# Weight pieces fetched by fewer DMAs, and half of w1 and w2 converted a step earlier, in an mLSTM cell with a multiplicative FFN

## The chip, the cores and the metric

The kernel runs on one core of a Trainium2 chip, as one program. The metric is the device time of one execution in microseconds; the median of several runs is given, and a profile of one execution goes with it. Times in the text without a unit of their own are microseconds (us) from the start of the profiled span.

## What is computed

An mLSTM cell over 4 batches, 8 heads, 768 time steps and a head size of 40, followed by a feed-forward block without a nonlinearity of its own, on the 3072 tokens:

```python
# mLSTM, per batch and head, t = 0 .. 767
m_new  = np.maximum(f_gate[t] + m, i_gate[t])
f_stab = np.exp(f_gate[t] + m - m_new);  i_stab = np.exp(i_gate[t] - m_new)
C = f_stab * C + i_stab * outer(v[t], k[t])        # 40 x 40
n = f_stab * n + i_stab * k[t]
y[t] = sigmoid(o_gate[t]) * (C @ q[t]) / max(abs(n @ q[t]), 1)

# FFN on x = y, 3072 tokens x 320
a = x @ w1;  b = x @ w2          # 320 x 1024 each
out = (a * b @ w3) @ w_out       # 1024 x 1024, 1024 x 320
```

The attention inputs are float32. The four weights arrive as float64: each value is two 32-bit words in memory, and the kernel makes float32 of them on the chip. So w3 is 8 MB to be read, w_out, w1 and w2 2.6 MB each.

## The kernel before

**Units and steps.** The sequence is cut into 24 units (6 pieces of 128 time steps x 4 batches). A loop over `s`, from 0 to 31, is written out in full (lines 737 to 831). In step `s` the kernel does the cell's matmuls of unit `s`, the outputs of unit `s-1`, brings the result of unit `s-2` into the layout of the FFN (xT), and adds FFN work as lists say: `n_up[s]` blocks of x @ w1 and x @ w2 (`up`, `up_rest`), `n_down[s]` output blocks (`ffn_out`), and from step 19 on a form of the up-projections with seven products in place of eight. The chunkwise cell needs k, q, v and the output gate of a unit; they are called for two steps ahead (`load`, `load_o`). From unit 10 on k and q are fetched by small DMAs in a form that VectorE turns (`load_turned`, 16 DMAs a unit), before that TensorE turns them.

**Weights.** A weight goes through four stations.

1. `fetch` (line 203) calls for a piece of raw 64-bit words by DMAs on SyncE's queue. The pieces stand in one list, `todo` (line 730): ten pieces of w1 and w2 (two halves of columns; in each half w1, w1, w2, w2 and the piece `wr` that holds the last 64 rows of both), eight pieces of w_out ("wo"), and sixteen parts of w3 (8 blocks of 128 rows, each in two parts of 64). `n_fetch[s]` says how many pieces shall have been called for by the end of step `s`; after step 7 it is four more than have been converted. The words go into a tile `raw` of 128 partitions, of which there are four; two pieces use the still unused memory of w3o instead (`idle`).
2. `scale` (line 179): ScalarE scales the high words (line 183) and the low words (line 187).
3. `convert` with `to_f32` (lines 230 and 189): VectorE puts the two together to a float32 (lines 191 and 192). For w3 it also turns 32 x 32 squares (line 241). `n_cvt[s]` says how many pieces are converted in step `s`. From step 9 on (`ahead`) two pieces are scaled a step before they are converted.
4. `fold` and `w3_mm`: TensorE multiplies the block of w3 by w_out into wp (16 matmuls per two parts), and ScalarE stores it as w3o. Since the FFN has no nonlinearity after a * b, w3 @ w_out is made once and used for all tokens.

**How pieces lie.** A piece of w_out is 128 rows that lie in four places of w_out, 32 rows each at distance 256 (`CQ`), one for each square of 32 partitions. A part of w3 is 64 rows; the columns are cut into four quarters, and quarter `j` goes to partitions 32j to 32j+31, with the two groups of 32 rows side by side in a partition. Before, each square of 32 partitions was fetched by its own DMA: 32 rows x 640 words for w_out, 32 rows x 2 groups x 512 words for w3.

**Order.** The instructions of each engine stand in the order in which the code makes them for the whole stretch up to step 32 (`keep_order`, `pinned`); TensorE has its order written out too (`in_order`). So an instruction that waits holds up all that stands behind it on its engine. SyncE issues all loads in one queue; in a step its order is: row of weights U of unit s+3 (`load_u`), k, q, v and gate of unit s+2, the turned loads of unit s+2, then the weight pieces. On ScalarE, the scaling of a step's weights stands at the end of the step, ahead of the copy of xT (line 468), of the evacuations `a_sb` (line 612) and of w3o (line 257) of the next.

Of the kernel before, what the change touches and what calls it, by code (L numbers as in the profile page):

```python
# [16 lines left out]
def kernel(  # L17
# [37 lines left out]
    DM = H * D  # L55
# [104 lines left out]
    wo = const.tile([128, FO, DM], FP, name="wo")  # L160
# [5 lines left out]
    w1_d, w2_d, w3_d, wo_d = (x.bitcast(U32) for x in (moe_w1, moe_w2, moe_w3, moe_w_out))  # L166
# [3 lines left out]
    def raw_tile(n, pieces):  # L170
        raw = idle.pop(0) if idle else wst.tile([128, n, 2], U32, name="raw", tag="raw", bufs=4)
        for r, src in pieces:
            dst = raw[r].rearrange("p n two -> p (n two)")
            if len(src.shape) == 3:
                dst = dst.rearrange("p (m n) -> p m n", m=2)
            nc.sync.dma_start(out=dst, in_=src)
        return raw

# [15 lines left out]
    def cols(c0, n):  # L194
        return slice(2 * c0, 2 * (c0 + n))
# [1 line left out]
    every = slice(0, 128)  # L197

    CQ = DFF // 4
    squares = [slice(32 * j, 32 * (j + 1)) for j in range(4)]  # L200
    pend, scaled = [], []

    def fetch(kind, i, part):

        if kind == "w12":
            c0 = part * CW
            if i < 2 * KF:
                wt, src = ((w1, w1_d), (w2, w2_d))[i // KF]
                ko = i % KF
                dst, pieces = wt[:, ko, c0:c0 + CW], [(every, src[ko * 128:(ko + 1) * 128, cols(c0, CW)])]  # L210
            else:
                dst, pieces = wr[:, c0:c0 + CW], [(slice(j * REM, (j + 1) * REM), src[KF * P:DM, cols(c0, CW)])
                                                  for j, src in enumerate((w1_d, w2_d))]
        elif kind == "wo":
            dst, pieces = wo[:, i, :], [(square, wo_d[j * CQ + i * 32:j * CQ + (i + 1) * 32, :])
                                        for j, square in enumerate(squares)]
        else:
            dst, pieces = None, [(square, w3_d[i * 128 + part * 64:i * 128 + (part + 1) * 64, cols(j * CQ, CQ)]
                                  .rearrange("(m r) n -> r m n", m=2)) for j, square in enumerate(squares)]
        pend.append((dst, raw_tile(dst.shape[-1] if dst is not None else CW, pieces), i, part))  # L220


# [269 lines left out]
    w3o_words = w3o.rearrange("p f d -> p (f d)").bitcast(U32).rearrange("p (n two) -> p n two", two=2)  # L492
    load(0, slice(0, 2))
    fetch("w12", 0, 0)
    load(0, slice(2, 3))
    fetch("w12", 1, 0)
    load(1, slice(0, 2))
    load_o(0)
    load(1, slice(2, 3))
    load_o(1)  # L500
    fetch("w12", 2, 0)
    idle += [w3o_words[:, i * CW:(i + 1) * CW] for i in range(2)]

# [224 lines left out]
    n_down = [0] * 17 + [2] * 6 + [1] * 7 + [0, 5]  # L728
    w12 = [("w12", i, part) for part in range(2) for i in range(2 * KF + 1)]
    todo = w12[3:] + [("wo", i, 0) for i in range(FO)] + [("w3", ko, part) for ko in range(FO) for part in range(2)]  # L730
    n_cvt = [0, 1, 1, 1, 1, 2, 4, 4, 4] + [2] * 7
    n_fetch = [4, 5, 6, 8, 10, 12, 16, 20]
    pinned, ahead = 32, 9
    behind = ExitStack()
    turned, converted, fetched = 0, 2, 3
# [126 lines left out]
```

## Time and profile before

| | |
|---|---|
| time, median of 3 runs | 451.98 us (450.0 to 457.32) |
| span of the profiled execution | 449.5 us |
| 16 DMA engines, share by queue | 50.5% for SyncE's loads (queue 1: 46.29 MB) |
| w3 parts: DMAs, size, issue to landing | 64, 128 KB, 3.3 us (median) |
| w_out pieces: DMAs, size, issue to landing | 32, 80 KB, 2.0 us (median) |
| k, v and gate: DMAs, size, issue to landing | 24 each, 160 KB, 4.5 to 4.8 us (median) |
| fetch of step 5, w_out | 64.26 us, 8 DMAs, 3.89 us of SyncE's time |
| fetch of step 6, w_out | 77.37 us, 16 DMAs, 8.57 us |
| fetch of step 7, w_out and w3 | 93.81 us, 16 DMAs, 3.58 + 4.20 us |
| fetch of step 8, w3 | 110.25 us, 16 DMAs, 8.24 us |
| fetch of step 9, w3 | 128.45 us, 8 DMAs, 3.69 us |
| fetch of step 13, w3, the last | 187.50 us, 8 DMAs, 3.60 us |

The fetches are read from the timeline of SyncE's queue: the first number is when SyncE begins to issue, the last how long it takes over the issues. A DMA's "issue to landing" runs from its own issue to the last of its completion signals. The busy share of the DMA engines is a mean over all 16; the profile doesn't list them one by one.

### The profile page before, as it was taken

The page shows a single profiled execution, that of the slowest core. Times are in us where ns is not written, and L with a number is a line of the kernel's source. Part 1 is how long each engine was busy: PE and PEld are TensorE (multiplying, and loading weights), DVE is VectorE, ACT ScalarE, POOL GpSimd, SP SyncE. Part 2 cuts the span into 40 slices and gives each one's busy share as a digit, 9 for nine tenths or more (in the row PEclk, how much of TensorE's full clock was granted, in tenths as well). Part 3 has the DMA queues.
Part 4 walks back from the last instruction along what each step waited for, and adds up shares of the span by engine and source line. Part 5 has one row for each costly group of instructions (what it writes and reads, how often), then busy time and mean ns, then how long its engine had stood idle before and what let it go on. Part 6 is the DMA issues. An engine that isn't in the chain of part 4 may idle for free.

```text
span 449.5 us, 12899 instructions
## 1 busy us (share of the span) xinstructions
PE 426.9 (95%) x5303; PEld 339.3 (75%) x5303; DVE 299.7 (67%) x629; ACT 150.9 (34%) x410; POOL 81.4 (18%) x155
## 2 busy tenths in 40 slices
PE   4988996999699999999999999999999999999997
PEld 3877875888577878878877878778778777777774
DVE  6375668478827866876685859678698776445800
ACT  4566557268442552353132312203111111001110
POOL 3434433033202211220222203202020000000000
PEclk9987999899989999999999999999999999999999
DMA  8999674569988695788444585563211120000001
GB/s 185 177 174 209 122 142 90 154 148 197 214 188 184 150 191 157 146 169 167 89 95 125 115 162 118 111 131 90 58 36 36 34 50 16 15 16 15 2 30 44
DMA packets 135595, 51.15 MB, mean 114 GB/s; under 512 B 109744, under 2 KB 127344, under 8 KB 135536
## 3 DMA queue, kind: packets, MB, share of 16 engines
q1 hardware_dynamic: 131936, 46.29, 50.5%
q10 hardware_dynamic: 3600, 4.03, 2.5%
q8 instruction: 41, 0.67, 0.6%
q14 instruction: 18, 0.15, 0.1%
HBM read 44.50 MB, written 5.80 MB: 112 GB/s over the span
## 4 chain that ended last, share of the span: by engine, by line
PE 85%; DVE 3%; issue 3%; ACT 3%; POOL 2%; DMA 2%; SPq 1%; POOLq 0%; DVEq 0%; ACTq 0%
PE cell L92 22%; PE pa L92 21%; PE pb L92 14%; PE po L92 14%; PE wp L92 7%; PE p L92 5%; PE pt L95 1%; DMA raw<-in_moe_w_dram 1%; PE px L95 1%; ACT pw L297 1%; POOL pw L302 1%; DMA q_all<-in_q_dram 1%; DVE pw L381 1%; DVE h L412 1%; POOL vw L324 1%
## 5 line engine op out<-in xcount | busy, mean ns | idle before, releaser
L92 PE MATMUL pa<-xT,w 128*128 128x256 f32 x240 | 61.9, 389 | 5.7 <-ACT xT L468 5.7
L92 PE MATMUL po<-w3o,ab 128*128 128x320 f32 x224 | 61.8, 433 | 0.0
L92 PEld LDWEIGHTS pa<-xT,w 128*128 128x128 f32 x240 | 45.4, 194 | 14.0 <-ACT xT L468 6.6
L92 PEld LDWEIGHTS po<-w3o,ab 128*128 128x128 f32 x224 | 42.4, 190 | 17.3 <-issue 0.4
L329 POOL TENSOR_TENSOR state<-state,decay 128x164 f32<-128x164 f32 x40 | 20.9, 523 | 173.9 <-DVE state L388 134.5
L92 PE MATMUL pb<-xT,w 128*128 128x256 f32 x192 | 47.8, 393 | 3.5 <-DVE w L192 3.5
L302 POOL TENSOR_SCALAR_AFFINE_SELECT pw<-pw 64x512 f32<-64x512 f32 x48 | 33.5, 697 | 64.3 <-ACT pw L297 50.9
L92 PEld LDWEIGHTS pb<-xT,w 128*128 128x128 f32 x192 | 37.9, 198 | 9.4 <-DVE w L192 3.9
L92 PE MATMUL cell<-w3o,ab 128*128 128x320 f32 x160 | 44.0, 432 | 0.0
L613 DVE TENSOR_TENSOR ab<-pb,a_sb 128x512 f32<-128x512 f32 x24 | 16.5, 689 | 39.2 <-ACT a_sb L612 39.2
L297 ACT ACTIVATE pw<-pw,aT 128x64 f32<-128x64 f32 x160 | 40.3, 340 | 2.8 <-ACT o_sb L715 2.8
L92 PEld LDWEIGHTS cell<-w3o,ab 128*128 128x128 f32 x160 | 30.4, 190 | 12.0
L612 ACT ACTIVATE a_sb<-pa 128x512 f32<-128x512 f32 x24 | 14.3, 597 | 70.6 <-PE pb L92 70.6
L92 PE MATMUL pa<-xT,wr 64*64 64x256 f32 x384 | 36.8, 386 | 1.1 <-DVE wr L192 1.1
L92 PE MATMUL pb<-xT,wr 64*64 64x256 f32 x384 | 36.2, 379 | 0.0
L660 DVE SCALAR_TENSOR_TENSOR a_sb<-pa,wo 128x512 f32<-128x512 f32 x12 | 8.3, 692 | 41.7 <-PE pa L92 41.7
L92 PE MATMUL wp<-wo,w3T 128*128 128x320 f32 x128 | 35.8, 432 | 0.0
L92 PEld LDWEIGHTS pa<-xT,wr 64*64 64x64 f32 x384 | 19.0, 132 | 16.0 <-issue 8.6
L92 PEld LDWEIGHTS wp<-wo,w3T 128*128 128x128 f32 x128 | 23.7, 190 | 8.9
L715 ACT COPY o_sb<-po 128x320 f32<-128x320 f32 x14 | 6.0, 426 | 67.4 <-PE po L92 63.5
L412 DVE TENSOR_TENSOR h<-cell,h 64x164 f32<-64x164 f32 x76 | 24.8, 326 | 1.4
L92 PEld LDWEIGHTS pb<-xT,wr 64*64 64x64 f32 x384 | 20.2, 133 | 3.0
(135 smaller groups left out, 732.9 us busy)
## 6 DMA issues: line engine op xcount, KB each, us to landing
raw<-in_moe_w_dram SPq DMA_DIRECT2D x64, 128.0 KB, 3.3
kbuf<-in_k_dram SPq DMA_DIRECT2D x24, 160.0 KB, 4.5
vbuf<-in_v_dram SPq DMA_DIRECT2D x24, 160.0 KB, 4.8
o_in<-in_o_gate_dram SPq DMA_DIRECT2D x24, 160.0 KB, 4.7
out_dram<-o_sb ACTq DMA_DIRECT2D x24, 160.0 KB, 1.8
raw<-in_moe_w_dram SPq DMA_DIRECT2D x7, 512.0 KB, 5.1
pw<-U_d SPq DMA_DIRECT2D x28, 128.0 KB, 3.6
raw<-in_moe_w_out_dram SPq DMA_DIRECT2D x32, 80.0 KB, 2.0
```

Source lines behind the costliest of these rows:

```text
L92: in_order(nc.tensor.matmul(out, lhsT=lhsT, rhs=rhs, start=start, stop=stop))
L95: in_order(nc.tensor.transpose(out, in_, ident[0:n, 0:n]))
L297: nc.scalar.activation(out=pw[:, h, :], in_=src[:, h, :], func=AF.Exp, bias=aT[:, c, b * H + h:b * H + h + 1])
L302: nc.gpsimd.affine_select(out=pw[r], in_=pw[r], compare_op=OP.is_ge, fill=0.0, base=0, pattern=[[0, H], [1, L]], channel_multiplier=-1)
L324: nc.gpsimd.tensor_tensor(out=vw_t[n], in0=vbuf[n % NBV], op=OP.mult, in1=wT[:, c, b * H:(b + 1) * H].unsqueeze(2).to_broadcast([P, H, D1]))
L329: nc.gpsimd.tensor_tensor(out=new, in0=old, op=OP.mult, in1=decay[:, b * NP:(b + 1) * NP, 2 * c + x:2 * c + x + 1] .to_broadcast([P, NP, D1]))
L381: first_read = nc.vector.tensor_tensor(out=pv, in0=ss, in1=pv, op=OP.mult)
L412: nc.vector.tensor_tensor(out=part, in0=ph[x][halves[e]], in1=part, op=OP.add)
L612: nc.scalar.mul(out=a_sb, in_=pa, mul=UP ** -2)
L613: nc.vector.tensor_tensor(out=ab_t[gr][j][:, fs[0]:fs[-1] + 1, t0:t0 + a_sb.shape[-1]], in0=pb, in1=a_sb, op=OP.mult)
L660: nc.vector.scalar_tensor_tensor(out=out, in0=p, scalar=UP ** -2, in1=q, op0=OP.mult, op1=OP.add)
L715: nc.scalar.copy(out=o_sb, in_=po)
```

## The change

A piece of w_out is now called for by one DMA in place of four, a part of w3 by two in place of four. The four squares of partitions are filled by one transfer: its destination is all 128 partitions, and its source is a view with the four places (`j`) as its outermost dimension, then 32 rows, then the words of a row. The two DMAs of a w3 part are its two groups of 32 rows. The bytes and the length of the contiguous rows (2,560 and 2,048 bytes) stay as they were. It saves SyncE the issuing of 56 DMAs.

Beside that, `n_cvt` and `n_fetch` are changed so that the second half of w1 and w2 is fetched and converted a step earlier: steps 4 to 6 convert 2, 2 and 3 pieces in place of 1, 2 and 4, and the fetches of steps 2 to 6 each reach one piece further, except that step 6 reaches the same count. From step 7 on both lists are as before.

```diff
     def raw_tile(n, pieces):
         raw = idle.pop(0) if idle else wst.tile([128, n, 2], U32, name="raw", tag="raw", bufs=4)
         for r, src in pieces:
-            dst = raw[r].rearrange("p n two -> p (n two)")
-            if len(src.shape) == 3:
-                dst = dst.rearrange("p (m n) -> p m n", m=2)
+            dst = (raw[:, r] if len(src.shape) == 3 else raw[r]).rearrange("p n two -> p (n two)")
             nc.sync.dma_start(out=dst, in_=src)
         return raw
...
-    squares = [slice(32 * j, 32 * (j + 1)) for j in range(4)]
...
         elif kind == "wo":
-            dst, pieces = wo[:, i, :], [(square, wo_d[j * CQ + i * 32:j * CQ + (i + 1) * 32, :])
-                                        for j, square in enumerate(squares)]
+            dst, pieces = wo[:, i, :], [(slice(0, DM), wo_d.rearrange("(j c) n -> j c n", j=4)[:, i * 32:(i + 1) * 32, :])]
         else:
-            dst, pieces = None, [(square, w3_d[i * 128 + part * 64:i * 128 + (part + 1) * 64, cols(j * CQ, CQ)]
-                                  .rearrange("(m r) n -> r m n", m=2)) for j, square in enumerate(squares)]
+            dst, pieces = None, [(slice(m * CQ, (m + 1) * CQ), w3_d[r0:r0 + 32, :].rearrange("r (j n) -> j r n", j=4))
+                                 for m, r0 in enumerate(range(i * 128 + part * 64, i * 128 + (part + 1) * 64, 32))]
...
-    n_cvt = [0, 1, 1, 1, 1, 2, 4, 4, 4] + [2] * 7
-    n_fetch = [4, 5, 6, 8, 10, 12, 16, 20]
+    n_cvt = [0, 1, 1, 1, 2, 2, 3, 4, 4] + [2] * 7
+    n_fetch = [4, 5, 7, 9, 11, 13, 16, 20]
```

## The prediction

> **What bounds the kernel now.** I read the page from the top (busy time, the 40 slices, the DMA queues), then the chain of waits in order of time, then the waits and the timeline where the chain leaves TensorE, last the windows of the DMA engines.
>
> ```profile
> PE 426.9 (95%) x5303; PEld 339.3 (75%) x5303; DVE 299.7 (67%) x629; ACT 150.9 (34%) x410; POOL 81.4 (18%) x155
> ...
> PE   4988996999699999999999999999999999999997
> ...
> PEclk9987999899989999999999999999999999999999
> DMA  8999674569988695788444585563211120000001
> ```
>
> TensorE is busy for 426.9 of 449.5 us. The dents lie in the first eleven slices (11.2 us each); from about 124 us the digit is 9 up to the tail, so whatever delays TensorE there is added to the time in full, and no change to the loads can gain there. What a faster start can give is bounded by the idle time before 124 us, and two waits in it concern the weights:
>
> ```profile
> PE pb L92 <- DVE w L192: 3.5, 1, 3.5
> ...
> PE pa L92 <- ACT xT L468: 5.7, 3, 4.2
> ...
> ACT raw L183 <- DMA raw<-in_moe_w_dram: 2.8, 3, 1.0
> ```
> ```profile
> 110.25 8.24 SPq L176 DMA_DIRECT2D raw<-in_moe_w_dram  x16
> ...
> 120.51 0.67 ACT L183 ACTIVATE raw<-raw 128x512 f32<-128x512 f32 x1 [0.99 <-DMA raw<-in_moe_w_dram]
> ...
> 123.76 0.46 ACT L468 COPY xT<-px 128x384 f32<-128x384 f32 x1
> ...
> 124.28 2.24 PE L92 MATMUL pa<-xT,w 128*128 128x256 f32 x7 [4.22 <-ACT xT L468]
> ```
>
> The first fence is of the waits (total, times, longest), the second of the timeline (start, us, what). The first wait is at 77.39 us: the second half of w2 isn't converted yet. The second, in step 9, is the interesting one: sixteen DMAs of w3 take SyncE 8.24 us to call for, ScalarE scales each piece when it lands, and behind the last scaling stands the copy of xT for which TensorE waits 4.22 us. The waits of that stage thus end with the landing of w3, and ScalarE is in order, so a later landing moves TensorE one for one.
>
> ```profile
> 113.00:118.00 5.00, 5.00 (x22) 3.79 (x21) 4.43 (x12) 1.25 (x2) 2.64 (x4) 1.00 0.81 221
> 171.00:176.00 5.00, 5.00 (x27) 4.13 (x30) 3.41 (x7) 0.00 (x0) 0.00 (x0) 1.00 0.44 132
> 128.00:143.40 15.40, 15.40 (x210) 12.42 (x209) 11.09 (x23) 6.51 (x17) 3.31 (x6) 0.97 0.84 187
> 143.40:158.80 15.40, 15.40 (x212) 12.48 (x212) 11.36 (x24) 6.50 (x17) 3.32 (x6) 1.00 0.72 172
> 200.00:231.00 31.00, 31.00 (x424) 25.10 (x423) 22.92 (x47) 8.67 (x27) 6.78 (x13) 1.00 0.62 126
> ```
>
> The last two columns are the mean busy share of the 16 DMA engines and GB/s. A step of the steady stage is 15.4 us (the chain of waits has the wp matmuls at 164.74, 180.17 and 195.60 us). The reader is to see that the engines are busy 72 to 84% in a step that fetches two parts of w3 and 62% in steps that fetch none: there is room on sixteen engines, not on a few of them.
>
> **What the Trainium skill says.** (1) "DMA: Bandwidth & Descriptors", section "Why a DMA increments its semaphore by 16 and not by 1": the number of engines k of a DMA is the largest number up to 16 that divides the size of the slowest dimension (other than 1) of both access patterns, and on this path the lowest-numbered k engines are taken. (2) The same page, "Rules for kernel authors": an outermost dimension under 16 confines the whole DMA to that many engines at most. The trace of before agrees as far as it goes:
>
> ```profile
> q1 hardware_dynamic: 131936, 46.29, 50.5%
> q10 hardware_dynamic: 3600, 4.03, 2.5%
> ...
> out_dram<-o_sb ACTq DMA_DIRECT2D x24, 160.0 KB, 1.8
> ...
> gates<-in_i_gate_dram ACTq DMA_DIRECT2D x3, 32.0 KB, 2.0
> ```
>
> Queue 10 carries 24 stores of 128 rows and 3 loads of 32 rows: 24 x (128+16) + 3 x (32+16) = 3600 packets, exactly with 16 completion packets per DMA, so both shapes ran on 16 engines. No DMA of before has an outer size under 32, so no run yet shows k under 16. (3) The page's "Specifications" price one engine at about 27 GiB/s (29 GB/s).
>
> **The change, part by part.**
>
> Fewer DMAs. Before: w_out 8 pieces x 4 and w3 16 parts x 4 = 96 DMAs; after: 8 x 1 and 16 x 2 = 40. SyncE is spared 56 issues of about 0.5 us (8.24 us for 16), some 28 us in all, mostly hidden; in step 9's fetch 4.1 us of issuing goes, which by itself would take away nearly all of the 4.22 us wait.
>
> The shape of those DMAs. Before, both sides of a DMA had 32 outermost. Now the source is 4 x 32 x row (j first) and the destination 128 x row. By (1) and (2) 4 is the largest number dividing 4 and 128, so all of w_out and w3 goes through four engines, which also carry their sixteenth of every other transfer, in the order of one queue. This is the step that decides, so I price it. One part of w3 is 512 KB, 131 KB per engine of the four. At the page's 29 GB/s that is 4.5 us; at what the windows show per busy engine (221/(16 x 0.81) = 17 GB/s, 132/(16 x 0.44) = 18.8) 7.7 to 7.0 us. A third way: two parts raise the engines' busy time per step from 0.62 x 15.4 = 9.5 to (12.9+11.1)/2 = 12.0 us, so 2.5 us for 66 KB, 26 GB/s. I take 25 GB/s, an estimate: 5.2 us a part; a piece of w_out (82 KB per engine) 3.3 us. The other transfers of a step: 9.5 us from the 200 to 231 us window; 7.0 if only its quieter half (215 to 231 us: share 0.44 of 16 us) is taken; I take 9.
>
> So a step with two parts puts 2 x 5.2 + 9 = 19.4 us on the four engines, against 15.4 us of compute: they become the bound. How long: the fetch of step 7 (93.81 us before, about 91 after, the wait of 3.5 us being gone) asks for 2 pieces of w_out and 2 parts of w3, step 8 for 4 parts, steps 9 to 13 for 2 each. To the last landing: 2 x 3.3 + 16 x 5.2 + 6 steps of other loads x 9 = 6.6 + 83.2 + 54 = 143.8 us, so 91 + 143.8 + 2 (landing, as the 2.0 us of w_out on the page) = 236.8 us. In before the last w3 piece is scaled here:
>
> ```profile
> 197.21 0.66 ACT L183 ACTIVATE raw<-raw 128x512 f32<-128x512 f32 x1
> 197.77 0.66 ACT L187 ACTIVATE raw<-raw 128x512 uint32<-128x512 uint32 x1
> 198.34 0.45 ACT L468 COPY xT<-px 128x384 f32<-128x384 f32 x1
> ```
>
> The shift is 236.8 - 197.2 = 39.6 us, gain of the early part included. It builds up so: in step 9 the fourth part lands at 91 + 6.6 + 10.4 + 9 + 20.8 + 2 = 139.8 us where before its scaling began at 122.66, 17 us; then 4 to 5 us in each of five steps (19.4 against 15.4). The ring does not run dry between, since SyncE calls for the next loads right behind each fetch and four raw buffers let two parts stand in the queue while two are converted. Queued behind the waiting scaling on ScalarE are the copy of xT, the evacuations a_sb and the w3o copy; TensorE waits for the first, VectorE (ab) for the second. After step 13 TensorE has no idle time in which to catch up.
>
> The second half of w1 and w2 one step earlier. No instruction more or less, and TensorE's and GpSimd's order is the same; on VectorE one conversion goes from step 6 to step 4. Gain: the 3.5 us wait at 77 us. Cost: one scaling (0.67 + 0.68 us) and conversion (0.85 + 1.0 us) more in step 4, where ScalarE and VectorE have gaps (ScalarE is idle 2.3 us before the kT copy at 58.01), and 512 KB called for one step earlier, at 20 to 40 us, where the DMA engines are full: 512 KB at the 177 GB/s of that stretch is 3 us on loads for k and v. Taken as 0 to 3 us, I take 1, within the rounding of the start at 91.
>
> Sum: 452.0 + 39.6 = 491.6, given as 491.
>
> **The rivals.** (B) Sixteen engines take the new DMAs, if what counts isn't the outermost 4. Then only the gains remain: 3.5 less 1 at 77 us and 4.2 at 124 us: 452.0 - 6.7 = 445.3, faster by 1.5%. For it: that step 9's wait is made of issue time. Against it: the page's rule. (C) Four engines, but hidden: if the rate is 29 GB/s and the other loads cost only 7.0 us, the sum is 2 x 2.8 + 16 x 4.5 + 6 x 7 = 119.6, last landing at 212.6, +15; with another step of slack from the buffers (loads are called for two steps ahead) it ends at 452. Between 450 and 460; against it, the windows' 17 to 19 GB/s. (D) Worse: at 17 GB/s and 9.5 us, 2 x 4.8 + 16 x 7.7 + 57 = 189.8, last landing at 282.8, +85.6: 537; for it, that the windows show this rate under load; against it, that twelve engines fall quiet and contend less.
>
> **How the numbers follow.** Forecast (the four engines bound steps 8 to 13) 0.78; B 0.12; C 0.06; D 0.04. The forecast's own spread follows from the bounds of its two costs, 4.5 to 7.7 us a part and 7.0 to 9.5 us a step, which are unlikely to lie at the same end together: 460 to 530. I give 456 to 532, which holds 0.95 of the forecast and about half of C and D, 0.79 in all, and leaves out B. Slower by over 2% (above 461) takes nearly all of the forecast and D: 0.79. Faster by over 2% needs 2.4 us more than B holds: 0.04. Within 2% is the rest, 0.17.
>
> **What would show it.** Packets in queue 1: 56 DMAs less are 896 completion packets less, so 131,040 if all run on 16 engines, and 40 x 12 = 480 less again, 130,560, if the new ones run on four. TensorE's digit should fall under 9 in the slices from about 110 to 240 us, with ScalarE L183 waiting for the DMA of w3 by tens of us in total (2.8 before), TensorE for xT and a_sb; the DMA share per window must drop while the wait grows. The wait at 77 us should be gone in either case. Wrong would be: 131,040 packets, or 130,560 with no longer waits of L183.

## The result, and the profile after

| | before | after |
|---|---|---|
| time, median of 4 runs | 452.02 us (450.0 to 457.32) | 494.38 us (489.14 to 497.79) |
| ratio after / before, 95% interval | | 1.0865 (1.0772 to 1.0958) |
| TensorE busy in the profiled span | 426.9 of 449.5 us | 440.2 of 496.1 us |

Some executions of either kernel run in a slower state; the ratios leave them out, so a median can stand higher than its ratio says, and since the profiled execution of after is one of them (497.79 us, the slowest of its four), nothing is built on a difference that it alone shows.

The page of after: busy times, slices (12.4 us each), and SyncE's queue.

```profile
PE 440.2 (89%) x5303; PEld 347.3 (70%) x5303; DVE 299.5 (60%) x629; ACT 151.8 (31%) x410; POOL 81.6 (16%) x155
...
PE   5989999990707798697999999999999999999997
...
PEclk9965999995857999997999999999999999999999
DMA  8999164535344554544477666566221111000001
...
q1 hardware_dynamic: 130560, 46.29, 42.2%
...
raw<-in_moe_w_dram SPq DMA_DIRECT2D x34, 256.0 KB
```

Three things are to be seen. Queue 1 carries 130,560 packets, the number forecast for four engines. The new dents of TensorE lie in slices 10 to 19, from 112 to 236 us, as forecast, where before had nines but for one 6, and the granted clock is low around the deepest of them. And the DMA digits in that stretch are 3 to 5, lower than in before (mostly 5 to 9), though TensorE now waits for the DMAs. A mean over 16 engines can't show that four of them are full. (The page of after has no landing times for SyncE's DMAs, and the chain of waits breaks off there into "issue"; the waits and the timeline have to be read in their place.)

The waits of after, in total, number and longest:

```profile
DVE ab L609 <- ACT a_sb L608: 64.7, 19, 18.1
...
ACT raw L181 <- DMA raw<-in_moe_w_dram: 52.9, 12, 7.8
...
PE pa L92 <- ACT xT L464: 31.1, 8, 18.0
...
PE px L95 <- ACT a_sb L608: 10.9, 1, 10.9
```

ScalarE waited 2.8 us for w3 before and 52.9 us now; TensorE's wait for xT went from 5.7 to 31.1 us, and a wait of 10.9 us (for a_sb, behind the scalings of step 8) is new. The 3.5 us wait for the converted w2 is gone. The timeline of step 9 shows how one becomes the other:

```profile
132.72 0.67 ACT L181 ACTIVATE raw<-raw 128x512 f32<-128x512 f32 x1 [7.78 <-DMA raw<-in_moe_w_dram]
138.00 0.65 ACT L181 ACTIVATE raw<-raw 128x512 f32<-128x512 f32 x1 [4.04 <-DMA raw<-in_moe_w_dram]
144.67 0.65 ACT L181 ACTIVATE raw<-raw 128x512 f32<-128x512 f32 x1 [5.45 <-DMA raw<-in_moe_w_dram]
150.13 0.65 ACT L181 ACTIVATE raw<-raw 128x512 f32<-128x512 f32 x1 [4.27 <-DMA raw<-in_moe_w_dram]
151.22 0.46 ACT L464 COPY xT<-px 128x384 f32<-128x384 f32 x1
151.74 3.58 PE L92 MATMUL pa<-xT,w 128*128 128x256 f32 x8 [17.99 <-ACT xT L464]
```

The four parts of w3 are scaled as they land. The gaps within a pair are 5.28 and 5.46 us, which is the time a part takes on its engines. The copy of xT stands behind the fourth, and TensorE has waited 17.99 us for it. From there on the fetches set the pace; SyncE's timeline of the weight fetches in steps 8 to 13:

```profile
124.93 12.30 SPq L174 DMA_DIRECT2D raw<-in_moe_w_dram  x8
...
141.08 5.66 SPq L131 DMA_DIRECT2D vbuf<-in_v_dram  x1
...
155.58 2.60 SPq L174 DMA_DIRECT2D raw<-in_moe_w_dram  x4
...
174.56 2.55 SPq L174 DMA_DIRECT2D raw<-in_moe_w_dram  x4
177.22 2.22 SPq L151 DMA_DIRECT2D pw<-U_d  x2
179.49 0.58 SPq L131 DMA_DIRECT2D kbuf<-in_k_dram  x1
180.11 4.21 SPq L131 DMA_DIRECT2D vbuf<-in_v_dram  x1
184.37 5.92 SPq L145 DMA_DIRECT2D o_in<-in_o_gate_dram  x1
190.33 2.08 SPq L140 DMA_DIRECT2D q_all<-in_k_dram  x4
192.46 1.86 SPq L140 DMA_DIRECT2D q_all<-in_q_dram  x4
194.43 2.63 SPq L174 DMA_DIRECT2D raw<-in_moe_w_dram  x4
...
214.38 2.65 SPq L174 DMA_DIRECT2D raw<-in_moe_w_dram  x4
...
233.26 2.63 SPq L174 DMA_DIRECT2D raw<-in_moe_w_dram  x4
```

Between the last five fetches lie (233.26 - 155.58)/4 = 19.42 us, against steps of 15.4 us before. SyncE itself is held up: one load of v keeps it 5.66 us, and the eight DMAs of step 8 take it 12.30 us, more than the sixteen of before (8.24 us). The step that is shown in full has v and gate at 4.21 and 5.92 us; in before they are

```profile
147.17 0.58 SPq L131 DMA_DIRECT2D vbuf<-in_v_dram  x1
147.80 2.56 SPq L145 DMA_DIRECT2D o_in<-in_o_gate_dram  x1
```

From 155.58 to 233.26 us SyncE never pauses for more than 0.11 us between two instructions.

### The profile page after: what moved, and what is told of

Same layout as the page of the kernel before. It is cut to its first block, busy times and chain, and to the rows that moved or that the text cites. A ratio compares the mean times of both kernels' runs of the same rounds, so it can differ in the third digit from the quotient of the medians.

```text
span 496.1 us, 12806 instructions
## 1 busy us (share of the span) xinstructions
PE 440.2 (89%) x5303; PEld 347.3 (70%) x5303; DVE 299.5 (60%) x629; ACT 151.8 (31%) x410; POOL 81.6 (16%) x155
## 3 DMA queue, kind: packets, MB, share of 16 engines
q1 hardware_dynamic: 130560, 46.29, 42.2%
## 4 chain that ended last, share of the span: by engine, by line
PE 59%; issue 18%; SPq 8%; DMA 7%; POOL 3%; ACT 2%; DVE 2%; DVEq 0%; POOLq 0%; ACTq 0%
PE cell L92 18%; PE po L92 12%; PE pa L92 12%; PE pb L92 7%; PE p L92 4%; DMA raw<-in_moe_w_out_dram 3%; SPq L131 3%; DMA raw<-in_moe_w_dram 3%; PE wp L92 2%; SPq L140 2%; POOL pw L298 1%; PE pt L95 1%; SPq L145 1%; DMA vbuf<-in_v_dram 1%; SPq L174 1%
## 5 line engine op out<-in xcount | busy, mean ns | idle before, releaser
L92 PE MATMUL pa<-xT,w 128*128 128x256 f32 x240 | 69.1, 424 | 31.1 <-ACT xT L464 31.1
L92 PEld LDWEIGHTS pa<-xT,w 128*128 128x128 f32 x240 | 49.2, 211 | 42.9 <-ACT xT L464 34.2
L92 PE MATMUL po<-w3o,ab 128*128 128x320 f32 x224 | 61.8, 433 | 0.0
L181 ACT ACTIVATE raw<-raw 128x512 f32<-128x512 f32 (+1 forms) x32 | 20.2, 631 | 72.6 <-DMA raw<-in_moe_w_dram 52.9
L92 PE MATMUL wp<-wo,w3T 128*128 128x320 f32 x128 | 37.8, 450 | 0.7 <-DVE ab L609 0.7
L92 PE MATMUL pa<-xT,wr 64*64 64x256 f32 x384 | 36.8, 386 | 0.0
L92 PEld LDWEIGHTS wp<-wo,w3T 128*128 128x128 f32 x128 | 24.8, 199 | 10.7 <-issue 1.4
```

What stands on the lines that cost most here:

```text
L92: in_order(nc.tensor.matmul(out, lhsT=lhsT, rhs=rhs, start=start, stop=stop))
L181: nc.scalar.activation(out=hi, in_=hi, func=AF.Prelu, scale=2.0 ** -111, alpha=2.0 ** 32)
```

## Experiments

Theory A is that of the prediction: the outermost 4 of the source confines each merged DMA to four engines, and their queue is the new bound. The rivals: B, the merged DMAs are slow (or fast) in themselves, by number and size; C, the lists of fetches and conversions cost the time. Before had medians of 454.3 to 456.1 us beside the experiments, so ratios are to be compared, not times.

### One half of the change at a time: e1_merge_only, e2_lists_only

```diff
 # e1: after, with the lists of before
-    n_cvt = [0, 1, 1, 1, 2, 2, 3, 4, 4] + [2] * 7
-    n_fetch = [4, 5, 7, 9, 11, 13, 16, 20]
+    n_cvt = [0, 1, 1, 1, 1, 2, 4, 4, 4] + [2] * 7
+    n_fetch = [4, 5, 6, 8, 10, 12, 16, 20]
 # e2: before, with the lists of after (the reverse edit)
```

> The merged DMAs alone, with the fetch and convert lists of before. Theory A (each merged DMA runs on four DMA engines, whose queue then takes 19.4 us of transfers per 15.4 us step): the slowdown is all there, and the 3.5 us wait at 77 us stays: 492 to 499. Rival C (the lists moved the early loads into a congested stretch, and that is what costs): near 452.

> The lists of after (second half of w1 and w2 one step earlier), with the four DMAs per piece of before. Theory A: the 3.5 us wait of TensorE for the converted w2 goes, less about 1 us for the fuller early queue: 449 (447 to 452). Rival C: 470 to 494.

Measured: e1 1.0972 (1.0886 to 1.1058) of before, median 498.49 us; e2 0.9875 (0.9787 to 0.9963), median 453.73 us. The slowdown is all in the merged DMAs, and C falls. The lists are a gain of about 1% with the DMAs of before; with the merged ones the ratios (1.0865 for after, 1.0972 for e1) say the same, but their intervals overlap. The waits of e2 show why it isn't more:

```profile
PE pa L92 <- ACT xT L468: 8.1, 3, 6.7
```

The wait for w2 at 77 us is gone, but the wait in step 9 has grown from 4.2 to 6.7 us: part of the time won is spent there, since the four parts of w3 are called for only 1.3 us earlier (at 108.99 us, 110.25 before).

### Same DMAs, sixteen engines: e3_sixteen

```diff
 # e3: after, with 128 consecutive rows as the source; the tile's index is passed along
...
-            dst, pieces = wo[:, i, :], [(slice(0, DM), wo_d.rearrange("(j c) n -> j c n", j=4)[:, i * 32:(i + 1) * 32, :])]
+            dst, pieces = wo[:, i, :], [(every, wo_d[i * 128:(i + 1) * 128, :])]
...
+            dst, pieces = None, [((every, slice(m * CQ, (m + 1) * CQ)), w3_d[i * 128:(i + 1) * 128, cols((2 * part + m) * CQ, CQ)])
+                                 for m in range(2)]
```

> After, but the source of each merged DMA is 128 consecutive rows (of w_out, or of a quarter of the columns of w3), so that both sides have 128 outermost; number of DMAs, bytes and row lengths are those of after. It leaves the right elements of w_out and w3 out of place, so the output is of other weights. Theory A: all 16 engines, 131,040 packets in queue 1, and only the gains are left: 445 (442 to 449). Rival B (big merged DMAs are slow in themselves, however many engines take them): 480 to 495.

Measured: 0.9816 (0.9745 to 0.9886). Its queue line, and the scaling in step 9 to be set beside that of after:

```profile
q1 hardware_dynamic: 131040, 46.29, 50.4%
```
```profile
107.15 3.72 SPq L174 DMA_DIRECT2D raw<-in_moe_w_dram  x8
...
114.25 0.67 ACT L181 ACTIVATE raw<-raw 128x512 f32<-128x512 f32 x1
...
118.97 0.69 ACT L181 ACTIVATE raw<-raw 128x512 f32<-128x512 f32 x1 [0.57 <-DMA raw<-in_moe_w_dram]
...
120.10 0.47 ACT L464 COPY xT<-px 128x384 f32<-128x384 f32 x1
```

The same eight DMAs of the same size now take SyncE 3.72 us, and the fourth part is scaled at 118.97 us, 11.8 us after the fetch began; in after it was 25.2 us (150.13 - 124.93). The number and size of the DMAs are therefore not the cost. With all engines, fewer issues do what the change was meant for: TensorE's waits for xT are 1.4 us in all, 8.1 in e2. In the times this gain isn't settled, since the intervals of e3 and e2 (0.9787 to 0.9963) overlap.

### Which pieces cost it: e7_w3_four, e4_wout_merged

Both have the lists of after; e7 merges the DMAs of w3 alone, e4 those of w_out alone, each with that piece's edit from the diff of the change.

> The lists of after and the merged w3 DMAs; w_out by four DMAs a piece as before. Theory A: on the four engines the two late w_out pieces (6.6 us) and the backlog of the earlier ones are missing, the sixteen w3 parts (83 us) stay: 484 (475 to 490). If w_out were the greater cost: under 470.

> The lists of after and the merged w_out DMAs; w3 by four DMAs a part as before. Theory A: eight pieces put 26 us on the four engines over steps 4 to 7, which with the other loads is about what the steps have time for; only a little backlog: 455 (449 to 461). Rival (w_out, being fetched while the early steps wait for k, q and v, costs as much as w3): 465 or more.

Measured: e7 1.077 (1.0711 to 1.083), median 488.86 us; e4 1.0119 (1.0064 to 1.0175), median 459.4 us. Against e2 (0.9875) that is 1.077/0.9875 = 1.091 for w3 and 1.0119/0.9875 = 1.025 for w_out, some 40 and 11 us. Both together are 1.0865/0.9875 = 1.100; that it is less than the sum lies within the intervals. In the traces w_out costs less than 11 us: from the first w_out fetch to the last of w3 e4 takes 134.6 us (63.27 to 197.89) and e2 128.1 (57.53 to 185.67), so 6.5 us; the other 5.7 us by which e4's profile is late are there before a merged DMA is called for.

### The number of engines as the dose: e5_w3_eight, e6_w3_two

```diff
 # e5: source 8 x 16 rows x 512 words
+   [((every, slice(m * CQ, (m + 1) * CQ)),
+     w3_d.rearrange("(g a h b) n -> g h a b n", g=4, a=8, h=2)[n % 4, n // 4 % 2, :, :, cols(n // 8 * CQ, CQ)])
+    for m in range(2) for n in (4 * i + 2 * part + m,)]
 # e6: two squares of partitions a DMA, source 2 x 32 rows x 512 words
+   [((slice(64 * t, 64 * (t + 1)), slice(m * CQ, (m + 1) * CQ)),
+     w3_d[r0:r0 + 32, cols(2 * t * CQ, 2 * CQ)].rearrange("r (j n) -> j r n", j=2)) for m, r0 in ... for t in range(2)]
```

> The lists of after, w_out by four DMAs a piece, w3 by two DMAs a part as in after, but each DMA's source has 8 groups of 16 rows as its outermost dimension (rows and a quarter of the columns that don't belong there: w3's elements are out of place, bytes and row lengths are kept). Theory A: eight engines, 2.6 us a part on each, 2 x 2.6 + 9 = 14.2 us per 15.4 us step, not the bound: 449 (445 to 458), time between two fetches 15.4 us, 131,168 packets in queue 1 (131,424 less 32 x 8). Rival (two groups of strided rows in one source are slow whatever the number of engines): 480 or more.

> The lists of after, w_out by four DMAs a piece, w3 by FOUR DMAs a part as in before, but each DMA covers two squares of partitions and one group of 32 rows, so that its source has 2 outermost; the output is right. Theory A: two engines, 10.4 us a part, 2 x 10.4 + 9 = 29.8 us between two fetches: 567 (540 to 600), though the number of DMAs is that of before. Rival (the number and size of DMAs counts, not the engines): 445 to 460.

| w3 source's outermost size | DMAs per part | packets in queue 1 | us between fetches, steps 9 to 13 | ratio to before |
|---|---|---|---|---|
| 32 (e2) | 4 | 131,936 | 15.0 | 0.9875 (0.9787 to 0.9963) |
| 8 (e5) | 2 | 131,168 | 15.3 | 1.0109 (1.0056 to 1.0162) |
| 4 (e7) | 2 | 131,040 | 19.55 | 1.077 (1.0711 to 1.083) |
| 2 (e6) | 4 | 131,040 | 29.9 | 1.2628 (1.2572 to 1.2684) |

(In e2, e5 and e7 the distances are 125.76 to 185.67, 131.27 to 192.58 and 145.84 to 224.04 us in four steps; in e6, 206.35 to 296.05 in three.) The packets are those of before less 16 for each DMA saved and less 16 - k for each of the new ones with k engines: 131,168 = 131,936 - 32 x 16 - 32 x 8, and so on; e6 has as many DMAs as before and 64 x 14 = 896 packets less. The first and the last of the fetches of e6 that are counted, and its waits:

```profile
206.35 10.76 SPq L174 DMA_DIRECT2D raw<-in_moe_w_dram  x8
...
296.05 12.41 SPq L174 DMA_DIRECT2D raw<-in_moe_w_dram  x8
```
```profile
ACT raw L181 <- DMA raw<-in_moe_w_dram: 138.1, 15, 13.4
...
PE pa L92 <- ACT xT L467: 103.0, 8, 39.3
```

B is out: with the number of DMAs of before, and smaller ones than in after, e6 is the slowest of all, at 573.43 us where A had 567. Two equations give the two costs of the prediction: with p for a part on four engines and L for the other loads, 2p + L = 19.55 and 4p + L = 29.9, so p = 5.2 and L = 9.2 us. (L is what a step takes beyond w3, whatever it consists of.) With eight engines p + L = 14.4 us stays under the step, and the distance of the fetches is that of compute.

The kept trace, which has the start and length of every packet, shows the dose directly. A row of w3 is a packet of 2,048 bytes. (Four in five packets of that size are w3's, the others rows of U.) Over the steps of the table the commonest number of them in flight at once, other than none, is 2 in e6 (0.65 of the time), 4 in e7 and in after (0.41 each) and 8 in e5 (0.21); in before it lies between 12 and 15. The median packet takes 84 or 85 ns in all five. So a packet of a merged DMA isn't slower; fewer of them run at once.

Yet e5 took 457.39 us (median) where 449 was expected, still within the stated range. Its waits point to step 8, whose four parts stand in the queue at once: TensorE's longest wait for xT, in the step after, is 12.0 us (6.7 in e2):

```profile
PE pa L92 <- ACT xT L467: 13.5, 3, 12.0
```

### Is it the queue or the one long wait: e11_after_scale_later

```diff
-    pinned, ahead = 32, 9
+    pinned, ahead = 32, 10
```

> After, with scaling ahead from step 10 on. Theory A (the queue of the four DMA engines sets the end, not one wait): TensorE's wait in step 9 gets shorter by about two parts (10.8 us), but the last part lands no earlier, so the time comes back in the next steps: 485 to 496. Rival (the long wait of step 9 is the loss in itself): 480 or less.

Measured: 1.0896 (1.0811 to 1.098); after had 1.0865. The median, 496.96 us, is just above the stated range, with before at 456.14 us beside it. The wait of step 9, and its waits in total:

```profile
135.21 3.78 PE L92 MATMUL pa<-xT,w 128*128 128x256 f32 x8 [6.43 <-ACT xT L464]
```
```profile
PE pa L92 <- ACT xT L464: 30.2, 8, 13.6
```

In step 9 TensorE now waits 6.43 us in place of 17.99, but in all 30.2 (31.1 in after). The wait moved to later steps, and the time stayed: from the fetch of step 7 to the last scaling it is 148.7 us (93.17 to 241.85), in after 149.5 (98.49 to 248.00). The loads of w3 set the end, whichever instruction happens to wait for them.

### Versions that keep all engines: e8_pairs, e9_scale_later, e10_pairs_scale_later

```diff
 # e8: two raw tiles side by side; one DMA for each square fetches both
-        raw = idle.pop(0) if idle else wst.tile([128, n, 2], U32, name="raw", tag="raw", bufs=4)
...
+                double[:] = [wst.tile([128, 2 * CW, 2], U32, name="raw", tag="raw", bufs=2)]
+                half[:] = [double[0][:, j * CW:(j + 1) * CW] for j in range(2)]
...
+            dst, pieces = None, [] if part else [(square, w3_d[i * 128:(i + 1) * 128, cols(j * CQ, CQ)]
+                                               .rearrange("(m r) n -> r m n", m=4)) for j, square in enumerate(squares)]
...
+    n_fetch = [4, 5, 7, 8, 10, 12, 16, 20]
 # e9: e2 with ahead = 10;  e10: e8 with ahead = 10
```

> A version with few DMAs on all engines: two raw tiles lie side by side, and one DMA per square of 32 partitions fetches two pieces of w_out or both parts of a w3 block (32 rows outermost, then 2 or 4 groups), so 16 DMAs for w_out and 32 for w3; lists as in after, but for the fetches of steps 3 to 5, which are one piece back since two tiles come free together. All the same elements as before. Theory A: 16 engines and half the issues: both waits of TensorE for weights gone, 445 (441 to 449).

> The lists of after with the four DMAs per piece of before, and scaling ahead of conversion from step 10 on in place of step 9, so that in step 9 only two w3 parts are scaled ahead of the copy of xT. Theory A (a landing becomes TensorE time because the scaling of the third and fourth part stands ahead of that copy on ScalarE): the two scalings with their waits, 4.5 us from 118.1 us on, leave the path to TensorE, whose wait for xT falls from 6.7 us to 2 to 3: 444 (440 to 448). If the wait were made by something else: 448 to 453, as without it.

> The version with 48 DMAs on 16 engines, with scaling ahead from step 10 on. There the first scaling of step 9 itself starts at 122.7 us, late because SyncE comes to the fetch only at 114.4 us, so only the two later scalings (2.3 us) leave the path: 449 (445 to 452).

Measured: e8 0.9922 (0.9887 to 0.9956), median 452.17 us; e9 0.9808 (0.9746 to 0.987), 445.8 us; e10 0.9838 (0.9777 to 0.99), 448.72 us. The expectation of e8 missed: 452.17 us against 445, and by ratio 0.9922 against 445/452 = 0.985. It issues half as many DMAs, on all engines (131,168 packets, 48 x 16 less), but the wait in step 9 is 6.5 us:

```profile
122.74 0.68 ACT L191 ACTIVATE raw<-raw 128x512 f32<-128x512 f32 x1 [6.18 <-DMA raw<-in_moe_w_dram]
```

Two parts now land together, so the first is ready as late as the second: it is scaled 8.3 us after its fetch begins (122.74 against 114.40) and 8.6 in e10 (113.51 against 104.95), in e2 4.6 (113.62 against 108.99). That the fetch itself comes only at 114.40 us belongs to that one execution: its fetch of step 4 is already at 64.74 us, while e10, the same up to step 9, has 54.32 and 104.95. The expectation of e10 took the late fetch for a property of the version, so its number came out on a ground that was wrong in part.

e9 leaves the DMAs of before and takes the scaling of the third and fourth part out of the way of the copy of xT: the longest wait for xT falls from 6.7 us in e2 to 2.3 us.

```profile
PE pa L92 <- ACT xT L468: 4.6, 4, 2.3
```

e9 and e10 have the best ratios of the versions that compute the reference's function, and beat before and after; the intervals of e9 and e2 (0.9787 to 0.9963) overlap, so how much of e9's gain is the later scaling isn't settled by the times. Neither the early w1 and w2 nor the later scaling needs a merged DMA.

## Why the prediction came out as it did

**Four engines, by the outermost size.** Right, and shown: 130,560 packets as forecast, the dose of e5, e7 and e6 in time and in packets in flight, and e3 as the control. What the Trainium skill says on k in "DMA: Bandwidth & Descriptors" (section "Why a DMA increments its semaphore by 16 and not by 1") held for 2, 4, 8 and 16. That the four are the lowest-numbered ones no run here shows.

**The two costs.** 5.2 us a part was taken. The landings are 5.3 to 5.5 us apart, the two dose steps give 5.2, and 64 packets of 84 ns are 5.4. The third way of pricing a part, from the difference of two stretches of before, was nearest: the rate per busy engine in a mixed stretch (17 to 19 GB/s) was too low, since in the kept trace a packet of 160 bytes takes 14 ns and one of 640 bytes 32 ns (medians in after), 11 and 20 GB/s, and one of 2,048 bytes 84 ns, 24 GB/s; the page's 29 GB/s was too high.

The period was put at 19.4 us and is 19.42, but the 9 us in it are right in part by luck. They were to be other loads in a queue that doesn't run dry, "since SyncE calls for the next loads right behind each fetch". It does run dry. Packets of w3 are in flight for some 12 us of a step of after. Then SyncE, held at v and the gate until 190.29 us in the step shown above, still has the eight turned loads to issue (3.9 us), and the next fetch stands behind them. For over 1 us of a step fewer than four packets are in flight on all sixteen engines together. How much time the four have left can be estimated from the mean share of 0.49 in this stretch:

```profile
155.58:233.26 77.68, 66.16 (x841) 51.91 (x840) 45.41 (x92) 26.53 (x68) 13.24 (x24) 0.94 0.49 128
```

w3 takes 2 x 5.4 = 10.8 us a step on each of the four. If the other loads take the same time on all sixteen, they take (0.49 x 16 x 19.42 - 4 x 10.8)/16 = 6.8 us, and the four are idle for 19.42 - 10.8 - 6.8 = 1.8 us. So the 9 us are, by this estimate, some 7 us of loads and 2 us of pauses. What bounds a step is a loop: the four engines hold up SyncE, and SyncE comes late to the next fetch.

**The start.** Too early by 2 to 7 us. The fetch of step 7 was put at 91 us. It came at 93.17 us in e11, which has the same instructions as after up to step 9, and at 98.49 in after. The 5.3 us between the two don't come from the change: the fetch of step 4, ahead of the first merged DMA, is at 55.59 us in e11 and at 60.26 in after, and it lies anywhere from 54.3 to 61.8 us in the nine profiles that have the same instructions up to there. What the sum took as nothing is w_out's backlog on the four engines: from the first w_out fetch to the fetch of step 7 it is 32.3 us in e2, 36.1 in e11 and 36.8 in after, so some 4 us.

**The end.** From the fetch of step 7 to the last landing the sum had 143.8 + 2 = 145.8 us; to the last scaling it is 148.7 us in e11 and 149.5 in after. With the later start, that scaling shifts by 44.6 us in e11 and 50.8 in after, against 39.6. The span grew by less, 40.4 and 46.6 us: in before the block of matmuls that needs this last xT began at 203.36 us, 6.2 us after the scaling, as TensorE had earlier work to do, and in after at 249.67 us, 1.7 us after it. Taking the shift of the last scaling for the shift of the end was thus off by 4 us the other way. That 491 lies so near to 494.38 is luck in part: two terms were too short, by 5 us together in e11, and one was too long by 4.

**SyncE.** Half wrong. The "some 28 us in all" that it was to be spared are 23.5 us where engines are free: the issues of w_out and w3 take SyncE 47.2 us in before and 23.8 in e3. In after they take 38.0 us, so 9.2 are spared, and some 7 us are lost again at v and the gate in each step of the steady stretch.

**The early half of w1 and w2.** The wait at 77 us went, as forecast. That part of it would come back in step 9 was not in the prediction, and e2 shows it.

**The prediction's own rivals.** Its B, sixteen engines, gave 445.3 us, which is near what e3 measured (median 446.63), but it is not what after does. Its C took both costs at their lower ends, 4.5 and 7.0 us, and its D both at their upper ends, 7.7 and 9.5 us; the dose steps have 5.2 and 9.2.

Left open: how the pauses of the four engines are divided within a step. The packets of the trace don't name their engine, so the 1.8 us rest on other loads being spread evenly.

## What to carry to other kernels

Before merging DMAs, look at the outermost size of both sides of the new transfer: if it is under 16, price the transfer by the few engines it runs on and add what they carry of everything else, step by step against the step's compute. A low mean DMA share is no sign of room; completion packets counted from the page (16 a DMA, or fewer) tell how many engines took part. And where the landing of a load becomes time on the bound engine through an in-order neighbour, moving that neighbour's instruction can be worth as much as a faster load: e9 came to 0.9808, e3 to 0.9816.

## What the runs showed that I had not expected

- A full queue on four engines stops the issuing engine too: SyncE stood 5.66 us over one load of v, which uses all sixteen engines and took 0.58 us to issue before. The hold follows the number of engines: in the four steps between the fetches of steps 9 and 13, v and the gate together keep SyncE 8.5 to 10.1 us a step in after, 5.7 to 6.3 in e5 and 1.8 to 3.1 in before.
- TensorE runs the same 5303 matmuls in 433.5 us of busy time in e7 and 434.3 in e11, 426.9 before. The granted clock is low around the long waits: 0.68 on average from 121 to 150 us in after, where the eight matmuls behind the wait of 17.99 us take 3.58 us and the next eight 1.89; and e6, with waits of 39 us, has a mean clock of 0.884. What this costs in time wasn't measured; in steps 9 to 13 TensorE has 4 us a step to spare (19.42 against 15.4). It makes busy time a poor measure of work done.

```profile
121.00:150.00 29.00, 10.82 (x35) 7.59 (x35) 13.25 (x26) 7.59 (x19) 3.31 (x6) 0.68 0.42 120
```
